# Decay attention and softplus network: the state's products in whole float32 beside the transposes

## The chip, the cores and the metric

The kernel runs on one core of a Trainium2 chip. The metric is the device time of one execution in microseconds (us). PE is the matmul engine, PEld its weight loads, ACT, DVE and POOL the scalar, vector and general engines, SP the queue that issues most transfers.

## What is computed

A causal attention with decay, by the recurrence below, feeds a two-layer network with softplus. Shapes: q, k, v are 4 x 8 heads x 768 positions x 64; the network has 3072 tokens, 512 inputs and 2048 hidden units. The weights arrive as float64, the rest as float32.

```python
for t in range(S):
    state = gamma[None, :, None, None] * state + np.einsum('bhd,bhe->bhde', k[:, :, t], v[:, :, t])
    y[:, :, t] = scale * np.einsum('bhd,bhde->bhe', q[:, :, t], state)
h = x @ w_in          # x: y with heads side by side
g = np.maximum(h, 0.0) + np.log1p(np.exp(-np.abs(h)))
out = g @ w_out
```

## The kernel before

**Units.** The recurrence is done in chunks of C = 128 positions. A unit is one chunk of one batch for half of the heads (HH = 4), so there are 4 x 6 x 2 = 48 units; `hf` is the half, `c` the chunk within a batch, NC = 6. A unit is computed as: load kn, qn, vn (128 positions on the partitions x 4 heads x 64), scale qn and vn by tables of the decay (`decay`, on POOL), transpose kn and qn on PE (`operands`, tile tp), multiply to scores sc = k q (`scores`), mask them (POOL), form y = state q + v scores (`outputs`, tile yp), and update the state: td += the sum over the chunk of k times v (`new_state`, tile pp). `stack_state` copies td into st, the form in which yp's matmuls read it. The products pp are needed for every chunk but the last of a batch: 40 of the 48 units.

**Two ways of precision.** The first WHOLE = 10 units use float32 matmuls as they are ("whole units"): pp is one matmul a head with kn as weights (64 columns) and vn as the moving operand (64 columns), L191. The other 38 ("split units", 30 of them with pp) split each operand into a high and a low float32r part and sum the products: kh is kn cast to float32r on ACT (L152), kl the rest on DVE (L153), vhl both parts of v. A head's pp is then two matmuls, kh with both parts of v (128 columns, L195) and kl with the high part (64 columns, L196). pp has a high and a low half, and td takes both on DVE, by L202 and L204.

**The network.** For each block of T = 256 tokens and each pair p of 128-wide slices of the hidden layer, `hidden` makes hp with 24 float32r matmuls (L286 to L288, xh and xl being the parts of y), ACT, DVE and POOL make the softplus parts gh and gl, and `second` adds into acc (L316 to L318). At the start each weight slice is converted from float64 words on ACT, DVE and POOL (`convert_weights`: L82, L87 and L91 on ACT, L92 on POOL).

**Order.** Units and network are interleaved by ticks: unit u has its parts at tick 4u plus an offset, by the table PARTS:

```python
PARTS = {-6: load_unit, -2: decay, 0: operands, 2: scores, 3: new_state, 5: stack_and_outputs}
```

The writing order is a hint: each engine's final order is set by a scheduler when the program is built. Each engine works through its own queue in that order and waits where an operand isn't there. tp, sc, pp and yp share three PSUM buffers of the tag "a", the network's tiles have their own.

Of the kernel before, what the change touches and what calls it, by code (L numbers as in the profile page):

```python
# [10 lines left out]
F32 = mybir.dt.float32  # L11
F32R = mybir.dt.float32r
# [3 lines left out]
ALU = mybir.AluOpType  # L16

P = 128
C = 128
# [3 lines left out]
WHOLE = 10  # L23
# [7 lines left out]
def decay_attention_then_softplus_ffn(ctx: ExitStack, tc: tile.TileContext, q, k, v, w_in, w_out, qtab, vtab, gtab, out):  # L31
    nc = tc.nc
    B, H, S, D = q.shape
    DM, DF = w_in.shape
    NC = S // C
# [3 lines left out]
    HH = H // 2  # L39
    NJ = HH // 2  # L40
# [3 lines left out]
    attn = ctx.enter_context(tc.tile_pool(name="attn", bufs=1))  # L44
# [5 lines left out]
    ps_a = ctx.enter_context(tc.tile_pool(name="ps_a", bufs=3, space=bass.MemoryType.PSUM))  # L50
# [42 lines left out]


    units = [(c // NC, c % NC, hf) for c in range(B * NC) for hf in range(2)]
    loads, live, state, xs = {}, {}, {}, {}
    lo, up = slice(0, D), slice(D, P)


# [20 lines left out]
    def operands(n):  # L120
        b, c, hf = units[n]
        kn, qn, vn = loads.pop(n)
        tp = ps_a.tile([P, 2, NJ, C], F32, name="tp", tag="a")
        for j in range(NJ):
            nc.tensor.transpose(tp[:, 0, j, :], kn[:, 2 * j:2 * j + 2, :], ident)  # L125
        for j in range(NJ):
            nc.tensor.transpose(tp[:, 1, j, :], qn[:, 2 * j:2 * j + 2, :], ident)  # L127
        if n < WHOLE:
            kw = attn.tile([P, NJ, C], F32, name="kw", tag="kh")
            qw = qws[n % 2]  # L130
            nc.scalar.copy(kw, tp[:, 0])
            nc.scalar.copy(qw[lo, 0], tp[lo, 1])
            nc.vector.tensor_copy(qw[up, 1], tp[up, 1])
            live[n] = [(kw, qw), kn, vn]
            return
        kq = kqs[n % 2]
        sides = ((0, lo, up), (1, up, lo))
        for par, own, oth in sides:
            nc.scalar.copy(kq[own, :2, par], tp[own])  # L139
            nc.scalar.copy(kq[oth, 1, par], tp[own, 1])  # L140
        for par, own, oth in sides:
            nc.vector.tensor_tensor(kq[oth, 0, par], tp[own, 0], kq[own, 0, par].bitcast(F32), op=ALU.subtract)  # L142
            nc.vector.tensor_tensor(kq[own, 2, par], tp[own, 1], kq[own, 1, par].bitcast(F32), op=ALU.subtract)

        vhl = attn.tile([P, HH, 2, D], F32R, name="vhl", tag="vhl", bufs=2)
        nc.scalar.copy(vhl[:, :, 0, :], vn)
        nc.vector.tensor_tensor(vhl[:, :, 1, :], vn, vhl[:, :, 0, :].bitcast(F32), op=ALU.subtract)
        kh = kl = None
        if c < NC - 1:
            kh = attn.tile([P, HH, D], F32R, name="kh", tag="kh")  # L150
            kl = attn.tile([P, HH, D], F32R, name="kl")
            nc.scalar.copy(kh, kn)  # L152
            nc.vector.tensor_tensor(kl, kn, kh.bitcast(F32), op=ALU.subtract)  # L153
        live[n] = [kq, vhl, kh, kl]

    def scores(n):
        kq = live[n][0]
# [23 lines left out]

    def new_state(n):
        b, c, hf = units[n]
        live[n].append(state[hf][0] if c else None)
        if c == NC - 1:
            return
        pp = ps_a.tile([D, HH, 2, D], F32, name="pp", tag="a")
        if n < WHOLE:
            kn, vn = live[n][1:3]
            for h in range(HH):  # L190
                nc.tensor.matmul(pp[:, h, 0, :], lhsT=kn[:, h, :], rhs=vn[:, h, :], start=True, stop=True)  # L191
        else:
            vhl, kh, kl = live[n][1:4]
            for h in range(HH):
                nc.tensor.matmul(pp[:, h], lhsT=kh[:, h, :], rhs=vhl[:, h], start=True, stop=False)  # L195
                nc.tensor.matmul(pp[:, h, 0, :], lhsT=kl[:, h, :], rhs=vhl[:, h, 0, :], start=False, stop=True)  # L196
        if c == 0:
            td = attn.tile([D, HH, D], F32, name=f"td{hf}")
            nc.vector.tensor_copy(td, pp[:, :, 0, :])
        else:  # L200
            td = state[hf][1]
            nc.vector.tensor_tensor(td, pp[:, :, 0, :], td, op=ALU.add)  # L202
        if n >= WHOLE:
            nc.vector.tensor_tensor(td, pp[:, :, 1, :], td, op=ALU.add)  # L204
        state[hf] = [None, td]

    def stack_state(n):
        b, c, hf = units[n]
        if c == NC - 1:
            return  # L210
        tdv = state[hf][1].rearrange("d (j p) e -> d p j e", p=2)
        if n + 2 < WHOLE:
            st = attn.tile([P, NJ, D], F32, name=f"st{hf}", bufs=2)
            nc.scalar.copy(st[lo], tdv[:, 0])
            nc.scalar.copy(st[up], tdv[:, 1])
            state[hf][0] = st
            return
        st = attn.tile([P, 2, NJ, D], F32R, name=f"st{hf}", bufs=2)
        od = attn.tile([D, NJ, D], F32R, name="od")
        nc.scalar.copy(st[lo, 0], tdv[:, 0])  # L220
        nc.scalar.copy(od, tdv[:, 1])
        nc.scalar.copy(st[up, 1], tdv[:, 1])
        nc.vector.tensor_tensor(st[up, 0], tdv[:, 0], st[lo, 0].bitcast(F32), op=ALU.subtract)
        nc.vector.tensor_tensor(st[lo, 1], tdv[:, 1], od.bitcast(F32), op=ALU.subtract)
        state[hf][0] = st

    def outputs(n):
        b, c, hf = units[n]
        kq, *rest, st = live.pop(n)
        i, off = divmod((n // 2) * C, T)  # L230
        if i not in xs:
            xs[i] = [ffn.tile([P, ND, T], F32R, name=nm) for nm in ("xh", "xl")]
        xh, xl = xs[i]
        yp = ps_a.tile([D, 2, NJ, C], F32, name="yp", tag="a")
        for j in range(NJ):
            for par in range(2):
                h = 2 * j + par
                o = yp[:, par, j, :]
                if c and n < WHOLE:
                    nc.tensor.matmul(o, lhsT=st[:, j, :], rhs=kq[1][:, par, j, :], start=True, stop=False)  # L240
                elif c:
                    nc.tensor.matmul(o, lhsT=st[:, par, j, :], rhs=kq[:, 1, par, j, :], start=True, stop=False)
                    nc.tensor.matmul(o, lhsT=st[:, par, j, :], rhs=kq[:, 2, par, j, :], start=False, stop=False)  # L243
                if n < WHOLE:
                    kn, vn, a = rest
                    nc.tensor.matmul(o, lhsT=vn[:, h, :], rhs=a[:, h, :], start=c == 0, stop=True)  # L246
                else:
                    vhl, kh, kl, ah, al = rest
                    nc.tensor.matmul(o, lhsT=vhl[:, h, 0, :], rhs=ah[:, h, :], start=c == 0, stop=False)  # L249
                    nc.tensor.matmul(o, lhsT=vhl[:, h, 0, :], rhs=al[:, h, :], start=False, stop=False)  # L250
                    nc.tensor.matmul(o, lhsT=vhl[:, h, 1, :], rhs=ah[:, h, :], start=False, stop=True)  # L251
        g = hf * NJ
        to = [(par, x[rows, g:g + NJ, off:off + C]) for x in (xh, xl) for par, rows in ((0, lo), (1, up))]
        for par, hi in to[:2]:
            nc.scalar.copy(hi, yp[:, par])  # L255
        for (par, low), (_, hi) in zip(to[2:], to[:2]):
            nc.vector.tensor_tensor(low, yp[:, par], hi.bitcast(F32), op=ALU.subtract)  # L257

    def stack_and_outputs(n):
        stack_state(n)  # L260
        outputs(n)


    PARTS = {-6: load_unit, -2: decay, 0: operands, 2: scores, 3: new_state, 5: stack_and_outputs}
    FIRST_TICK = min(PARTS)
    PERIOD = 4
    last_tick = PERIOD * (len(units) - 1) + max(PARTS)
    per_block = PERIOD * 2 * NT

    def tick(n):  # L270
        for at, part in PARTS.items():
            u, r = divmod(n - at, PERIOD)
            if r == 0 and 0 <= u < len(units):
                part(u)
# [64 lines left out]
    def ticks_for(i):  # L339

        return min(per_block * (i + 1) + max(PARTS) - PERIOD + 1 + AHEAD, last_tick + 1)

# [40 lines left out]
    for a, b in zip(starts, starts[1:]):  # L383
        i = steps[b][0]
        if i == 2:
            a = b - TURN
# [59 lines left out]
```

## Time and profile before

| | |
|---|---|
| median of 3 runs | 701.77 us (700.23 to 701.84) |
| the profiled execution | 700.03 us, span 698.2 us |
| PE busy | 684.4 us (98%) |
| DVE, ACT, POOL busy | 433.2, 372.1, 281.4 us |
| granted PE clock | full |

The span is the time from the first to the last instruction of the profiled execution. A row of the profile names the source line (L286), the engine, the operation, output tile <- input tiles, shapes and a count. In rows in order of time the first two numbers are the start and the duration in us; rows of groups end with the busy time of all and the mean duration of one in ns, then the idle time before them. A float32 matmul may show as two records. An entry like "[0.17 <-issue]" gives idle time ahead of the row and what ended it.

### The profile page before, as it was taken

What the parts mean: (1) busy time and instruction counts of PE and PEld (TensorE: products, weight loads), DVE (VectorE), ACT (ScalarE), POOL (GpSimd) and SP (SyncE); (2) the same over time, 40 slices, a digit from 0 to 9 for tenths busy, and PEclk for the clock granted to TensorE, in tenths of its full rate; (3) what the DMA queues carried; (4) which work ended last, traced back from release to release, by engine and by line L of the source; (5) the groups of instructions that cost most, each with busy time, mean ns of one, the idle gap of its engine ahead of it and who ended that gap; (6) DMA issues with size and microseconds to landing.
All of it is one profiled execution on the core that took longest, in us unless ns stands there. A gap on an engine that the chain in (4) does not pass through costs nothing.

```text
span 698.2 us, 13537 instructions
## 1 busy us (share of the span) xinstructions
PE 684.4 (98%) x5056; PEld 621.3 (89%) x5056; DVE 433.2 (62%) x893; ACT 372.1 (53%) x835; POOL 281.4 (40%) x324
## 2 busy tenths in 40 slices
PE   6899999999999999999999999999999999999997
PEld 4688889899999999999999999999999999999996
DVE  4676785557666766557667666647766676544221
ACT  6988885446556546445555555445555544543221
POOL 5676667334343342343334333433433333222221
PEclk9999999999999999999999999999999999999999
DMA  9976650122112112111111111211211110000000
GB/s 266 287 201 173 192 159 1 31 61 69 31 23 69 31 25 61 31 31 54 39 23 37 49 38 24 61 37 25 62 24 39 54 31 16 31 1 1 31 1 30
DMA packets 90752, 42.82 MB, mean 61 GB/s; under 512 B 77376, under 2 KB 85568, under 8 KB 90688
## 3 DMA queue, kind: packets, MB, share of 16 engines
q1 hardware_dynamic: 90240, 41.96, 22.2%
q8 instruction: 40, 0.66, 0.4%
q14 instruction: 24, 0.20, 0.1%
q10 hardware_dynamic: 448, 0.01, 0.0%
HBM read 35.66 MB, written 6.29 MB: 60 GB/s over the span
## 4 chain that ended last, share of the span: by engine, by line
PE 96%; ACT 1%; issue 0%; DVE 0%; ACTq 0%
PE hp L286 14%; PE hp L287 13%; PE hp L288 13%; PE acc L316 13%; PE acc L317 13%; PE acc L318 13%; PE sc L171 3%; PE tp L125 1%; PE tp L127 1%; PE pp L195 1%; PE yp L250 1%; PE yp L251 1%; PE yp L249 1%; PE yp L246 1%; PE yp L240 1%; PE yp L243 1%
## 5 line engine op out<-in xcount | busy, mean ns | idle before, releaser
L286 PE MATMUL hp<-xh,winhl 128*128 128x256 f32 x768 | 221.4, 289 | 0.4 <-ACT xh L255 0.4
L288 PE MATMUL hp<-xh,winhl 128*128 128x256 f32 x768 | 217.9, 284 | 0.0
L287 PE MATMUL hp<-xl,winhl 128*128 128x256 f32 x768 | 217.6, 283 | 0.0
L302 POOL TENSOR_TENSOR gl<-sp,gh 128x512 fp32r<-128x512 f32 x96 | 125.4, 1306 | 149.3 <-ACT gh L300 86.7
L316 PE MATMUL acc<-wouthl,gh 128*128 128x512 f32 x384 | 154.3, 402 | 0.0
L317 PE MATMUL acc<-wouthl,gh 128*128 128x512 f32 x384 | 150.4, 392 | 0.0
L318 PE MATMUL acc<-wouthl,gl 128*128 128x512 f32 x384 | 149.1, 390 | 0.0
L286 PEld LDWEIGHTS hp<-xh,winhl 128*128 128x128 f32 x768 | 146.5, 191 | 2.8 <-issue 0.5
L287 PEld LDWEIGHTS hp<-xl,winhl 128*128 128x128 f32 x768 | 147.0, 191 | 1.6 <-issue 0.5
L288 PEld LDWEIGHTS hp<-xh,winhl 128*128 128x128 f32 x768 | 146.8, 191 | 0.6 <-issue 0.3
L293 DVE TENSOR_SCALAR sp<-hp 128x512 uint32<-128x512 uint32 x96 | 66.1, 690 | 70.6 <-PE hp L288 61.0
L300 ACT CAST gh<-sp 128x512 fp32r<-128x512 f32 x96 | 59.5, 620 | 74.1 <-PE acc L317 57.4
L117 POOL TENSOR_TENSOR qn<-qn,qtabs 128x256 f32<-128x256 f32 x48 | 29.4, 613 | 151.1 <-DMA qn<-in_q_dram 125.0
L294 ACT ACTIVATE sp<-sp 128x512 f32<-128x512 f32 x96 | 60.9, 634 | 49.0 <-DVE sp L293 48.7
L318 PEld LDWEIGHTS acc<-wouthl,gl 128*128 128x128 f32 x384 | 71.9, 188 | 15.6
L316 PEld LDWEIGHTS acc<-wouthl,gh 128*128 128x128 f32 x384 | 72.4, 189 | 12.5 <-issue 0.5
L317 PEld LDWEIGHTS acc<-wouthl,gh 128*128 128x128 f32 x384 | 72.5, 189 | 11.4
L298 DVE SCALAR_TENSOR_TENSOR sp<-hp,sp 128x512 f32<-128x512 f32 x96 | 65.9, 687 | 12.8 <-ACT sp L294 11.6
L142 DVE TENSOR_TENSOR kq<-tp,kq 64x256 fp32r<-64x256 f32 x76 | 32.1, 422 | 67.0 <-ACT kq L140 65.8
L139 ACT CAST kq<-tp 64x512 fp32r<-64x512 f32 x76 | 44.1, 581 | 40.0 <-PE tp L127 38.8
L255 ACT CAST xh<-yp 64x256 fp32r<-64x256 f32 x96 | 35.1, 366 | 51.0 <-PE yp L251 44.5
L257 DVE TENSOR_TENSOR xl<-yp,xh 64x256 fp32r<-64x256 f32 x96 | 39.9, 416 | 33.7 <-ACT xh L255 32.7
(85 smaller groups left out, 1082.6 us busy)
## 6 DMA issues: line engine op xcount, KB each, us to landing
win<-in_moe_w_in_dram SPq DMA_DIRECT2D x16, 512.0 KB, 4.5
wout<-in_moe_w_out_dram SPq DMA_DIRECT2D x16, 512.0 KB, 4.4
kn<-in_k_dram SPq DMA_DIRECT2D x48, 128.0 KB, 2.3
qn<-in_q_dram SPq DMA_DIRECT2D x48, 128.0 KB, 2.8
vn<-in_v_dram SPq DMA_DIRECT2D x48, 128.0 KB, 2.2
out_dram<-o SPq DMA_DIRECT2D x24, 256.0 KB, 2.1
gtab_sb<-in_gtab_dram ACTq DMA_DIRECT2D x2, 2.0 KB, 3.8
qtabs<-in_qtab_dram ACTq DMA_DIRECT2D x1, 4.0 KB, 2.4
```

The source lines that it names most:

```text
L139: nc.scalar.copy(kq[own, :2, par], tp[own])
L286: nc.tensor.matmul(hp[:, k], lhsT=wt[:, 0, d, :], rhs=xh[:, d, :], start=d == 0, stop=False)
L287: nc.tensor.matmul(hp[:, k], lhsT=wt[:, 0, d, :], rhs=xl[:, d, :], start=False, stop=False)
L288: nc.tensor.matmul(hp[:, k], lhsT=wt[:, 1, d, :], rhs=xh[:, d, :], start=False, stop=d == ND - 1)
L293: nc.vector.tensor_scalar(sp.bitcast(U32), hps[s].bitcast(U32), 0x80000000, None, op0=ALU.bitwise_or)
L294: nc.scalar.activation(sp, sp, AF.Softplus)
L298: nc.vector.scalar_tensor_tensor(g, hps.pop(s), 0.0, g, op0=ALU.max, op1=ALU.add)
L300: nc.scalar.copy(gh, g)
L302: nc.gpsimd.tensor_tensor(gl, sps.pop(s), gh.bitcast(F32), op=ALU.subtract)
L316: nc.tensor.matmul(acc[i][t], lhsT=gh[:, k, ts], rhs=wt[:, 0], start=begins and k == 0, stop=False)
L317: nc.tensor.matmul(acc[i][t], lhsT=gh[:, k, ts], rhs=wt[:, 1], start=False, stop=False)
L318: nc.tensor.matmul(acc[i][t], lhsT=gl[:, k, ts], rhs=wt[:, 0], start=False, stop=ends and k == 1)
```

## The change

All units take the state's products from whole float32 kn and vn, one matmul a head (L132 in the new numbering). The products are written in `operands`, directly after the transposes; the td add follows in the same tick (0 in place of 3), since `new_state` is now called behind `operands`. kh, kl, the low half of pp and the second td add are gone. The state that `outputs` reads is kept in a table `prior` of its own.

```diff
+        if c < NC - 1:
+            pp[n] = ps_a.tile([D, HH, D], F32, name="pp", tag="a")
+            for h in range(HH):
+                nc.tensor.matmul(pp[n][:, h, :], lhsT=kn[:, h, :], rhs=vn[:, h, :], start=True, stop=True)
         if n < WHOLE:
-            kw = attn.tile([P, NJ, C], F32, name="kw", tag="kh")
+            kw = attn.tile([P, NJ, C], F32, name="kw")
...
-        kh = kl = None
-        if c < NC - 1:
-            kh = attn.tile([P, HH, D], F32R, name="kh", tag="kh")
-            kl = attn.tile([P, HH, D], F32R, name="kl")
-            nc.scalar.copy(kh, kn)
-            nc.vector.tensor_tensor(kl, kn, kh.bitcast(F32), op=ALU.subtract)
...
     def new_state(n):
         b, c, hf = units[n]
-        live[n].append(state[hf][0] if c else None)
+        prior[n] = state[hf][0] if c else None
         if c == NC - 1:
             return
-        pp = ps_a.tile([D, HH, 2, D], F32, name="pp", tag="a")
-        if n < WHOLE:
-            kn, vn = live[n][1:3]
-            for h in range(HH):
-                nc.tensor.matmul(pp[:, h, 0, :], lhsT=kn[:, h, :], rhs=vn[:, h, :], start=True, stop=True)
-        else:
-            vhl, kh, kl = live[n][1:4]
-            for h in range(HH):
-                nc.tensor.matmul(pp[:, h], lhsT=kh[:, h, :], rhs=vhl[:, h], start=True, stop=False)
-                nc.tensor.matmul(pp[:, h, 0, :], lhsT=kl[:, h, :], rhs=vhl[:, h, 0, :], start=False, stop=True)
...
-            nc.vector.tensor_tensor(td, pp[:, :, 0, :], td, op=ALU.add)
-        if n >= WHOLE:
-            nc.vector.tensor_tensor(td, pp[:, :, 1, :], td, op=ALU.add)
+            nc.vector.tensor_tensor(td, pp.pop(n), td, op=ALU.add)
...
+    def operands_and_state(n):
+        operands(n)
+        new_state(n)
+
-    PARTS = {-6: load_unit, -2: decay, 0: operands, 2: scores, 3: new_state, 5: stack_and_outputs}
+    PARTS = {-6: load_unit, -2: decay, 0: operands_and_state, 2: scores, 5: stack_and_outputs}
```

The change moves instructions in three places that matter here. First, PE in a split unit of the steady part. Before, the last two of the four heads' products, between other matmuls:

```order
L195 MATMUL pp<-vhl,kh 64x128
L196 MATMUL pp<-vhl,kl 64x64
L195 MATMUL pp<-vhl,kh 64x128
L196 MATMUL pp<-vhl,kl 64x64
L286 MATMUL hp<-xh,winhl 128x256
L287 MATMUL hp<-xl,winhl 128x256
```

and now:

```order
L280 MATMUL hp<-xh,winhl 128x256
L125 MATMUL tp<-ident,kn 128x128 x2
L127 MATMUL tp<-ident,qn 128x128 x2
L132 MATMUL pp<-vn,kn 64x64 x4
L308 MATMUL acc_2746<-wouthl,gh 128x512
L309 MATMUL acc_2746<-wouthl,gh 128x512
```

Eight float32r matmuls that stood by themselves have become four float32 ones between the transposes and the network's matmuls.

Second, PE among the whole units. Before, sc parts the runs of yp and pp:

```order
L318 MATMUL acc_684<-wouthl,gl 128x512
L246 MATMUL yp<-ah,vn 64x128
L163 MATMUL sc<-qw,kw 128x128 x4
L191 MATMUL pp<-vn,kn 64x64 x4
L286 MATMUL hp<-xh,winhl 128x256
```

Now pp stands directly ahead of the previous unit's yp (here its first rows), and sc by itself further on:

```order
L278 MATMUL hp<-xh,winhl 128x256
L132 MATMUL pp<-vn,kn 64x64 x4
L228 MATMUL yp<-qw,st_368 64x128
L234 MATMUL yp<-ah,vn 64x128
L228 MATMUL yp<-qw,st_368 64x128
```

pp and yp, both with 64 columns of weights, have become one run, which sc no longer parts.

Third, ACT ahead of the third pair of xh casts, which the network's first matmul needs. Before:

```order
L131 COPY kw<-tp 128x256
L132 COPY qw<-tp 64x256
L82 ACTIVATE win<-win 128x512
L91 CAST winhl<-w 128x512
L87 ACTIVATE wp<-wout 128x512
L82 ACTIVATE wout<-wout 128x512
L255 CAST xh<-yp 64x2x128 x2
```

and now:

```order
L82 ACTIVATE wout<-wout 128x512
L91 CAST wouthl<-w 128x512
L87 ACTIVATE wp<-win 128x512
L82 ACTIVATE win<-win 128x512
L201 COPY st_368<-td_183 64x128
L202 COPY st_368<-td_183 64x128
L91 CAST winhl<-w 128x512
L87 ACTIVATE wp<-wout 128x512
L82 ACTIVATE wout<-wout 128x512
L243 CAST xh<-yp 64x2x128 x2
```

More weight conversions and one more unit's st copies have moved ahead of that pair.

More of the change, by code (lines that the diff above doesn't have):

```diff
@@ L95, in decay_attention_then_softplus_ffn @@
     units = [(c // NC, c % NC, hf) for c in range(B * NC) for hf in range(2)]
-    loads, live, state, xs = {}, {}, {}, {}
+    loads, live, pp, prior, state, xs = {}, {}, {}, {}, {}, {}
     lo, up = slice(0, D), slice(D, P)
@@ L133, in operands @@
             nc.vector.tensor_copy(qw[up, 1], tp[up, 1])
-            live[n] = [(kw, qw), kn, vn]
+            live[n] = [(kw, qw), vn]
             return
@@ L147, in operands @@
         nc.vector.tensor_tensor(vhl[:, :, 1, :], vn, vhl[:, :, 0, :].bitcast(F32), op=ALU.subtract)
-        kh = kl = None
-        if c < NC - 1:
-            kh = attn.tile([P, HH, D], F32R, name="kh", tag="kh")
-            kl = attn.tile([P, HH, D], F32R, name="kl")
-            nc.scalar.copy(kh, kn)
-            nc.vector.tensor_tensor(kl, kn, kh.bitcast(F32), op=ALU.subtract)
-        live[n] = [kq, vhl, kh, kl]
+        live[n] = [kq, vhl]
     def scores(n):
@@ L183, in new_state @@
         b, c, hf = units[n]
-        live[n].append(state[hf][0] if c else None)
+        prior[n] = state[hf][0] if c else None
         if c == NC - 1:
             return
-        pp = ps_a.tile([D, HH, 2, D], F32, name="pp", tag="a")
-        if n < WHOLE:
-            kn, vn = live[n][1:3]
-            for h in range(HH):
-                nc.tensor.matmul(pp[:, h, 0, :], lhsT=kn[:, h, :], rhs=vn[:, h, :], start=True, stop=True)
-        else:
-            vhl, kh, kl = live[n][1:4]
-            for h in range(HH):
-                nc.tensor.matmul(pp[:, h], lhsT=kh[:, h, :], rhs=vhl[:, h], start=True, stop=False)
-                nc.tensor.matmul(pp[:, h, 0, :], lhsT=kl[:, h, :], rhs=vhl[:, h, 0, :], start=False, stop=True)
         if c == 0:
             td = attn.tile([D, HH, D], F32, name=f"td{hf}")
-            nc.vector.tensor_copy(td, pp[:, :, 0, :])
+            nc.vector.tensor_copy(td, pp.pop(n))
         else:
             td = state[hf][1]
-            nc.vector.tensor_tensor(td, pp[:, :, 0, :], td, op=ALU.add)
-        if n >= WHOLE:
-            nc.vector.tensor_tensor(td, pp[:, :, 1, :], td, op=ALU.add)
+            nc.vector.tensor_tensor(td, pp.pop(n), td, op=ALU.add)
         state[hf] = [None, td]
@@ L228, in outputs @@
         b, c, hf = units[n]
-        kq, *rest, st = live.pop(n)
+        kq, *rest = live.pop(n)
+        st = prior.pop(n)
         i, off = divmod((n // 2) * C, T)
@@ L244, in outputs @@
                 if n < WHOLE:
-                    kn, vn, a = rest
+                    vn, a = rest
                     nc.tensor.matmul(o, lhsT=vn[:, h, :], rhs=a[:, h, :], start=c == 0, stop=True)
                 else:
-                    vhl, kh, kl, ah, al = rest
+                    vhl, ah, al = rest
                     nc.tensor.matmul(o, lhsT=vhl[:, h, 0, :], rhs=ah[:, h, :], start=c == 0, stop=False)
```

## The prediction

> **What bounds the kernel now.** I read the page's shares first, then three stretches of the span, then the order of time on PE around the state's products.
>
> Rows of the page (busy time and share of the span of each engine; the chain that ended last, by engine):
>
> ```profile
> span 698.2 us, 13537 instructions
> PE 684.4 (98%) x5056; PEld 621.3 (89%) x5056; DVE 433.2 (62%) x893; ACT 372.1 (53%) x835; POOL 281.4 (40%) x324
> PEclk9999999999999999999999999999999999999999
> PE 96%; ACT 1%; issue 0%; DVE 0%; ACTq 0%
> ```
>
> PE's busy time in three stretches (window, its length, PE busy and its matmuls, granted clock):
>
> ```profile
> 0.00:28.00 28.00, 18.27 (x114) 1.00 1.04 282
> 28.00:690.00 662.00, 662.00 (x4927) 1.00 0.19 52
> 690.00:698.20 8.20, 4.08 (x18) 1.00 0.17 64
> ```
>
> From 28 us to 690 us PE is never idle. So the end moves by what PE's stream gains or loses there, plus any shift of the moment at which the stream becomes full; work taken from ACT and DVE (53% and 62% busy) is worth nothing by itself. A group's mean duration says little here, since matmuls overlap: a 128x256 hp lasts 0.28 us and the next starts 0.12 us later. I therefore price by starts: from the last big matmul ahead of a small group to the second big one behind it, minus the usual pace of the two (hp 0.12 us, acc 0.22 us as between its rows below).
>
> **The split units' products, before.** PE in order of time at one split unit (start, duration):
>
> ```profile
> 230.83 0.39 PE L317 MATMUL acc<-wouthl,gh 128*128 128x512 f32 x1
> 231.06 0.39 PE L318 MATMUL acc<-wouthl,gl 128*128 128x512 f32 x1
> 231.28 0.22 PE L195 MATMUL pp<-vhl,kh 128*64 128x128 f32 x1
> 231.34 0.19 PE L196 MATMUL pp<-vhl,kl 128*64 128x64 f32 x1
> 231.37 0.25 PE L195 MATMUL pp<-vhl,kh 128*64 128x128 f32 x1
> ...
> 231.69 0.19 PE L196 MATMUL pp<-vhl,kl 128*64 128x64 f32 x1
> 231.72 0.36 PE L286 MATMUL hp<-xh,winhl 128*128 128x256 f32 x1
> 231.92 0.28 PE L287 MATMUL hp<-xl,winhl 128*128 128x256 f32 x1
> ```
>
> From 231.06 to 231.92 are 0.86 us; less 0.22 and 0.12, the eight float32r matmuls of a unit cost 0.52 us. There are 30 such units:
>
> ```profile
> L195 PE MATMUL pp<-vhl,kh 128*64 128x128 f32 x120 | 17.2, 243 | 0.0
> L191 PE MATMUL pp<-vn,kn 128*64 128x64 f32 x80 | 7.4, 237 | 0.0
> ```
>
> 120 records at four a unit are 30 units; and the ten whole units' 40 float32 matmuls leave 80 records, so a whole float32 matmul runs as two passes.
>
> **The same products in whole float32.** Whole units already do what the change makes all units do. Half a unit's products (two heads, four passes) stand alone between hp matmuls, and a full unit's (eight passes) a little earlier:
>
> ```profile
> 70.56 0.28 PE L287 MATMUL hp<-xl,winhl 128*128 128x256 f32 x1
> 70.77 0.45 PE L191 MATMUL pp<-vn,kn 128*64 128x64 f32 x4
> 71.15 0.39 PE L288 MATMUL hp<-xh,winhl 128*128 128x256 f32 x1
> 71.37 0.28 PE L286 MATMUL hp<-xh,winhl 128*128 128x256 f32 x1
> ```
>
> ```profile
> 61.23 0.68 PE L191 MATMUL pp<-vn,kn 128*64 128x64 f32 x8
> ```
>
> From 70.56 to 71.37, less twice 0.12, four passes cost 0.57 us. Four more lengthen the run by 0.68 - 0.45 = 0.23 us, so a pass takes 0.058 us in the stream, and 0.57 - 0.23 = 0.34 us is a fixed toll of the run. The rows show where it falls: pp starts 0.21 us after hp instead of 0.12, the first hp behind it comes late, and the second follows after 0.22 instead of 0.12. A unit's eight passes then cost 0.57 + 0.23 = 0.80 us where the float32r group costs 0.52.
>
> The change puts them behind the transposes, which are float32 too. Does that spare the toll? The nearest rows have transposes followed at once by one float32 matmul of 64 columns of weights (yp), two passes:
>
> ```profile
> 27.70 0.51 PE L286 MATMUL hp<-xh,winhl 128*128 128x256 f32 x2 [0.37 <-ACT xh L255]
> 28.04 0.39 PE L125 MATMUL tp<-ident,kn 128*128 128x128 f32 x2
> 28.26 0.38 PE L127 MATMUL tp<-ident,qn 128*128 128x128 f32 x2
> 28.57 0.43 PE L240 MATMUL yp<-qw,st 128*64 128x128 f32 x2
> 28.93 0.38 PE L287 MATMUL hp<-xl,winhl 128*128 128x256 f32 x1
> 29.16 0.28 PE L288 MATMUL hp<-xh,winhl 128*128 128x256 f32 x1
> ```
>
> A pair of transposes takes 0.22 us (28.04 to 28.26), so yp would start at 28.48 and starts at 28.57; its pair takes 0.43 where a transposes' pair takes 0.38, 0.05 more; hp behind it is 0.09 late (0.36 between the two starts, 0.22 for two passes and the 0.05), and the next comes 0.23 later instead of 0.12. Together 0.34 us: the full toll. It goes with 64-column float32 weights, not with float32 as such; a float32 score matmul with 128 columns pays none (40.10 to 40.44 is two passes of 0.11 and one hp of 0.12):
>
> ```profile
> 40.10 0.38 PE L163 MATMUL sc<-qw,kw 128*128 128x128 f32 x2
> 40.24 0.36 PE L288 MATMUL hp<-xh,winhl 128*128 128x256 f32 x1
> 40.44 0.28 PE L286 MATMUL hp<-xh,winhl 128*128 128x256 f32 x1
> ```
>
> So a split unit's group goes from 0.52 to 0.80 us: 30 x 0.28 = **+8.4 us**, all in the stretch where PE is full. Ends: 30 x (0.46 - 0.52) = -1.8 if behind the transposes only the eight passes of 0.058 counted, and +8.4 with the full toll. I take +8.4, since the yp rows show the very transition.
>
> Weight loads show the toll's place: float32r weights load one matmul early, the float32 ones of yp only with their own matmul.
>
> ```profile
> 231.06 0.13 PEld L195 LDWEIGHTS pp<-vhl,kh 128*64 128x64 f32 x1
> 28.57 0.19 PEld L240 LDWEIGHTS yp<-qw,st 128*64 128x64 f32 x2 [0.17 <-issue]
> ```
>
> The Trainium skill ("TensorE: Matmul & The Clock Gate", the step on LDWEIGHTS) says that the queue pulls weight loads ahead, so that the next tile's weights load while this tile's matmul runs. By that rule the product's first load would hide behind the transposes and the split units would gain a little (the rival "no toll"). The float32r row agrees with it, the yp row does not.
>
> **Whole units.** Their matmuls are the same, but their runs join: before, pp mostly stood behind sc, which ends one 64-column run and begins another; now it stands next to yp, and the two are one run. The order lists 23 runs of 64-column float32 matmuls after the first hp and up to the last whole unit's yp before, and 12 now. 11 x 0.34 = **-3.7 us**. Ends: 0, if PE's gaps there are set by waits, and -3.7; PE is full there, so I take the whole.
>
> **The start.** The first hp (27.70 above) needs the third pair of xh casts, and ACT reaches it late: in the new order 48 ACT instructions stand from the first kw copy up to that pair, before 40 (six more weight conversions, two more st copies). ACT's stretch before, its first row and its end, with two conversions in a row:
>
> ```profile
> 5.91:26.90 20.99, 17.76 (x40) 1.00 1.15 314
> ```
>
> ```profile
> 5.91 0.37 ACT L131 COPY kw<-tp 128x256 f32<-128x256 f32 x1 [3.81 <-PE tp L127]
> ...
> 24.73 0.63 ACT L87 ACTIVATE wp<-wout 128x512 uint32<-128x512 uint32 x1
> 25.30 0.67 ACT L82 ACTIVATE wout<-wout 128x512 f32<-128x512 f32 x1
> 26.90 0.74 ACT L255 CAST xh<-yp 64x256 fp32r<-64x256 f32 x2 [0.93 <-PE yp L246]
> ```
>
> Conversions follow each other at 0.57 us (24.73 to 25.30); with 0.3 for an st copy, an estimate, eight more are 6 x 0.57 + 2 x 0.3 = 4.0 us. ACT is idle for 20.99 - 17.76 = 3.2 us there, which could absorb as much: +0.8 to +4.0. One more unit's transposes (2 x 0.22) are by then behind PE, so +0.4 to +3.6. On PE each pp now stands ahead of the previous unit's yp and of its own sc, and waits for its vn; on POOL the second unit's vn now stands behind a weight subtraction:
>
> ```profile
> 11.88 1.28 POOL L92 TENSOR_TENSOR winhl<-w,winhl 128x512 fp32r<-128x512 f32 x1
> ```
>
> That may add 1.3, so the end is +4.9; I take **+2.5**, near the middle, as such a wait keeps part of ACT's idle time alive. PE cannot give this back later, being full.
>
> **At nothing.** Gone are, per split unit, kh (ACT), kl and one of the two td adds (DVE); PE's full stretch covers them, and if it didn't, ACT and DVE would be faster, not slower. The td add comes three ticks earlier and needs the st copies of two units ago, which were issued three ticks earlier still. kn and vn are kept no longer than the end of pp or yp, so the loads on SP's queue keep their distance; tp, pp, yp and two sc share three PSUM buffers as before, five allocations a unit, which in the steady part stand 96 rows of PE's order apart from the next unit's. The last two units have no product, and the tail after 690 us stays.
>
> **Sum.** 8.4 - 3.7 + 2.5 = +7.2 us on the profiled execution's 700.03 us: 707.2. That execution is 1.7 below the median of the runs (701.77) and beside the fastest (700.23); for a median I add half of it, **708.1 us**.
>
> **Rivals.**
> - *No toll behind transposes.* The place is the first pass of pp behind tp, the price 30 x 0.34; it decides if PE runs tp and pp as one float32 stretch. Sum -1.8 - 3.7 + 2.5 = -3.0: 697.0 and, as a median, 697.9, faster. For it: transposes and products are both float32 from the same kn. Against it: the 28.57 row. With half the toll, 30 x 0.17 = 5.1 come back, and the kernel is within 0.3% of before.
> - *No gain in the whole units, and a start that waits fully.* The scheduler's order has one whole unit's last head parked far behind its first three, and pp now waits in PE's queue. +8.4 + 4.9 - 0 = +13.3: about 714. For it: ACT is 85% busy ahead of the first hp; against it: PE is full from 28 us on, so the tolls there are not waits.
> - *A start that loses nothing.* ACT's idle 3.2 us takes up the conversions: 8.4 - 3.7 + 0.4 = +5.1: 706 as a median.
>
> **Chances.** Forecast (+5.5 to +10) 0.62; the start without loss 0.18; whole units without gain 0.10; no toll 0.06 and half the toll 0.04. About 0.3% (2.1 us) is what a measurement of this kernel tells from no change. So slower 0.90, same 0.04, faster 0.06. The range takes the forecast, both starts and most of the whole-unit rival: 703.5 to 713.
>
> **What would show it.** In the new profile: pp as 320 records of 64 columns; behind each second transposes' pair a gap of 0.09 us, eight passes in 0.46 us, and acc twice 0.1 late, 0.80 us in all. If acc follows after the usual pace the toll step is wrong. The first hp comes near 30.6 us instead of 27.70 (the start), with PE full from then on, and 12 tolls instead of 23 up to the last whole unit's yp. The prediction fails if the toll is shared with the transposes, or if a wait appears on PE inside the full stretch.

## The result and the profile after

The changed kernel takes 708.76 us (median of 4 runs, 708.19 to 709.15); the kernel before took 701.67 us beside it. The ratio is 1.0105 with a 95% interval of [1.0088, 1.0123]: slower by 1%, and 0.7 us above the forecast of 708.1. The profiled execution took 708.19 us, 8.16 more than that of before. Beside this run and the experiments the kernel before took 699.9 to 700.4 us in some executions and 701.2 to 702.5 us in the others; its profiled execution (700.03) is of the first kind, so a difference from it comes out larger than one between medians.

The page of the changed kernel, the same rows as of before:

```profile
span 706.5 us, 13405 instructions
PE 689.5 (98%) x5056; PEld 625.2 (88%) x5056; DVE 394.8 (56%) x833; ACT 358.0 (51%) x805; POOL 279.9 (40%) x324
PE 94%; ACT 1%; DVE 0%; issue 0%; ACTq 0%
```

DVE has 38 us less to do and ACT 14, and the span is 8.3 us longer: on engines with a third or half of their time free the saving bought nothing. PE busy rose by 5.1 us; the other 3.2 us are idle time, which the stretches place (window, length, PE busy, DVE, ACT and POOL after PEld, granted clock):

```profile
0.00:28.00 28.00, 15.44 (x96) 12.71 (x97) 14.09 (x35) 20.78 (x44) 17.62 (x32) 0.91 1.04 281
28.00:690.00 662.00, 661.47 (x4896) 601.92 (x4895) 377.93 (x795) 334.49 (x757) 259.68 (x291) 1.00 0.19 52
```

From 28 us on PE is as good as full: 0.53 us of its 662 are idle, where before none were. Ahead of that it does 15.44 us of work instead of 18.27, at a granted clock of 0.91 instead of 1.00, so some 2.8 us of the added idle time lie there.

One split unit of the changed kernel, PE in order of time (start, duration):

```profile
236.63 0.28 PE L280 MATMUL hp<-xh,winhl 128*128 128x256 f32 x1
236.75 0.38 PE L125 MATMUL tp<-ident,kn 128*128 128x128 f32 x2
236.97 0.38 PE L127 MATMUL tp<-ident,qn 128*128 128x128 f32 x2
237.28 0.68 PE L132 MATMUL pp<-vn,kn 128*64 128x64 f32 x8
237.89 0.50 PE L308 MATMUL acc<-wouthl,gh 128*128 128x512 f32 x1
238.22 0.39 PE L309 MATMUL acc<-wouthl,gh 128*128 128x512 f32 x1
238.45 0.39 PE L310 MATMUL acc<-wouthl,gl 128*128 128x512 f32 x1
```

After the second pair of transposes pp would start at 237.19 and starts at 237.28: 0.09 us. From pp to acc are 0.61 us where eight passes of 0.058 are 0.46, so 0.15 more, and from the first acc to the second 0.33 instead of 0.23. Together the 0.34 of the toll. From 236.63 to 238.22, less one hp (0.12) and one acc (0.23), tp and pp cost 1.24 us; tp alone costs 0.44, so pp costs 0.80. All 160 matmuls show as two records each, and the first weight load of a unit's pp (PEld) starts only with its matmul:

```profile
L132 PE MATMUL pp<-vn,kn 128*64 128x64 f32 x320 | 28.3, 233 | 5.4 <-POOL vn L118 4.5 <-DVE xl L245 0.5 <-POOL qn L117 0.2
237.28 0.54 PEld L132 LDWEIGHTS pp<-vn,kn 128*64 128x64 f32 x8 [0.17 <-issue]
```

### The profile page after: what moved, and what is told of

Its sections match the earlier page's. It is cut to its first block, busy times and chain, and to the rows that moved or that the text cites. A ratio compares the mean times of both kernels' runs of the same rounds, so it can differ in the third digit from the quotient of the medians.

```text
span 706.5 us, 13405 instructions
## 1 busy us (share of the span) xinstructions
PE 689.5 (98%) x5056; PEld 625.2 (88%) x5056; DVE 394.8 (56%) x833; ACT 358.0 (51%) x805; POOL 279.9 (40%) x324
## 4 chain that ended last, share of the span: by engine, by line
PE 94%; ACT 1%; DVE 0%; issue 0%; ACTq 0%
PE acc L308 13%; PE hp L278 13%; PE hp L279 13%; PE hp L280 13%; PE acc L309 12%; PE acc L310 12%; PE pp L132 3%; PE sc L170 3%; PE yp L237 1%; PE tp L125 1%; PE tp L127 1%; PE yp L238 1%; PE yp L239 1%; PE yp L230 1%; PE yp L231 1%; PE yp L228 1%
## 5 line engine op out<-in xcount | busy, mean ns | idle before, releaser
L176 POOL TENSOR_SCALAR_AFFINE_SELECT ah<-ah 128x512 fp32r<-128x512 f32 (+1 forms) x48 | 30.5, 635 | 85.5 <-DVE al L173 76.6
```

## The experiments

Each was compared with the kernel before on the same chip; for e1 to e4 that was at 701.45 us, for e5 to e7, on another chip, at 701.27. In the diffs, "..." and comments stand for code left out.

### e1: the precision alone

```diff
-    PARTS = {..., 0: operands_and_state, 2: scores, 5: ...}
+    PARTS = {..., 0: operands, 2: scores, 3: products_and_state, 5: ...}
     # products: the four float32 matmuls of a unit, moved out of operands
```

> Precision alone: the products of all units are whole float32, but stay at tick 3 as in the kernel before, away from the transposes. PE's order up to the tenth unit is that of before. Theory (a toll of 0.34 us of every run of 64-column float32 matmuls, whatever stands beside it): the 30 split units cost 0.80 instead of 0.52 us each, the start and the whole units are as before: 8.4 us over the kernel before, about 710.1, the first hp near 27.7 us. Rival (what the changed kernel lost comes from the place next to the transposes: the wait for vn in PE's queue and the order there): within 2 us of the kernel before.

Measured: 709.1 us, ratio 1.0109 [1.0091, 1.0127], 7.6 us over the kernel before. The products stand by themselves between other matmuls, and a unit's group reads:

```profile
234.05 0.39 PE L314 MATMUL acc<-wouthl,gh 128*128 128x512 f32 x1
234.28 0.39 PE L315 MATMUL acc<-wouthl,gl 128*128 128x512 f32 x1
234.60 0.68 PE L184 MATMUL pp<-vn,kn 128*64 128x64 f32 x8
235.21 0.39 PE L283 MATMUL hp<-xh,winhl 128*128 128x256 f32 x1
235.43 0.28 PE L284 MATMUL hp<-xl,winhl 128*128 128x256 f32 x1
```

From 234.28 to 235.43 are 1.15 us, less 0.23 and 0.12: 0.80, the same as behind the transposes. So the split units lose through the format, wherever they stand. The rival, that the place does it, is out. The total fell 1.0 us short of the theory's 710.1, and the first hp came at 29.35 us where 27.7 was expected (the last section shows why). From the first hp to the end of the span, which leaves the start out, the profiled execution of e1 takes 679.45 us and that of the kernel before 670.50: 8.95 more, with 8.4 expected.

### e2: the place alone

```diff
+        if n < WHOLE and c < NC - 1:      # in operands, behind the transposes
+            pp = pps[n] = ps_a.tile([D, HH, 2, D], F32, name="pp", tag="a")
+            for h in range(HH):
+                nc.tensor.matmul(pp[:, h, 0, :], lhsT=kn[:, h, :], rhs=vn[:, h, :], start=True, stop=True)
     # split units as before: kh, kl and vhl at tick 3
```

> Place alone: the ten whole units' products stand next to the transposes as in the changed kernel, the split units keep their float32r products with kh and kl at tick 3. Theory: the start loses 3.4 us as in the changed kernel (first hp near 31.5 us), 12 runs of 64-column float32 matmuls stand where 23 stood, 11 x 0.34 = -3.7; together about -0.3: 701.4, no change. Rival (the joined runs save nothing, as the gaps were waits): +3.4, 705.1. Rival (the start's loss belongs to the split units' change): -3.7, 698.

Measured: 701.09 us, ratio 0.9997 [0.9987, 1.0006]: no change. The start is lost as in the changed kernel (the first hp is at 32.31 us, where 31.5 was expected), although the split units are as before, so the rival that the split units' change delays it is out. Something of about the same size must have come back in the whole units. Eleven tolls less, 3.7 us, are of that size; had the joined runs saved nothing, 705.1 was to be expected. The trace shows it directly. Counted from the first hp to the last whole unit's yp, the kernel before has 23 runs of 64-column float32 matmuls, e2 and the changed kernel have 12 each. One joined run of e2:

```profile
49.32 0.68 PE L132 MATMUL pp<-vn,kn 128*64 128x64 f32 x8
49.84 0.38 PE L244 MATMUL yp<-qw,st 128*64 128x128 f32 x2
...
51.37 0.38 PE L250 MATMUL yp<-ah,vn 128*64 128x128 f32 x2
51.68 0.39 PE L300 MATMUL hp<-xl,winhl 128*128 128x256 f32 x1
51.90 0.28 PE L301 MATMUL hp<-xh,winhl 128*128 128x256 f32 x1
```

Between pp and yp nothing is lost: 0.52 us for eight passes and the first pass's 0.05. From the first hp to the end of the span are 667.09 us against 670.50 before. Of the 3.41 us gained 0.44 are transposes that now stand ahead of the first hp; the other 3.0 are what the whole units save, less 0.4 us of waits that PE did not have there before.

### e3: the first four units back at tick 3

```diff
+LATE = 4
+        if n >= LATE:        # in operands, behind the transposes
+            products(n)
+    # units below LATE: products(n) and new_state(n) at tick 3
```

> The changed kernel with the products of the first four units back at tick 3, all else as changed; the order up to the first hp is that of before. Theory: the first hp comes at 27.7 us again and the start's 3.4 us are gone; 11 runs of 64-column float32 matmuls where 23 stood, -4.1; split units +8.4: +4.3 over the kernel before, 706.0. Rival (the late first hp was a delay that other work used up, so nothing comes back): as the changed kernel, 708.8.

Measured: 705.85 us, ratio 1.0063 [1.0047, 1.008]: 4.4 us over the kernel before, where 4.3 was expected, and 2.9 less than the changed kernel's 708.76 (which ran on another occasion; by the two ratios it is also 2.9). Of the 2.9, 0.34 is one toll fewer (11 against 12), so some 2.6 us are the start. The first hp is at 28.91 us where 27.7 was expected; in this profiled execution the granted clock was 0.53 from 24 to 26 us, as in the one of e1 that the last section shows.

### e4: who sets the first hp?

```diff
-        nc.gpsimd.tensor_tensor(vn, vn, vtabs[...], op=ALU.mult)
+        if n != 3:
+            nc.gpsimd.tensor_tensor(vn, vn, vtabs[...], op=ALU.mult)
```

In the changed kernel PE stands still for 3.15 us ahead of the fourth unit's pp, for vn on POOL (start, duration, idle time before and what ended it):

```profile
22.17 0.44 PE L127 MATMUL tp<-ident,qn 128*128 128x128 f32 x2 [0.43 <-POOL qn L117]
25.77 0.78 PE L132 MATMUL pp<-vn,kn 128*64 128x64 f32 x8 [3.15 <-POOL vn L118]
...
31.52 0.50 PE L278 MATMUL hp<-xh,winhl 128*128 128x256 f32 x2
```

That looks like the cause of the late first hp. This kernel takes the wait away.

> The changed kernel, but the fourth unit's v is not scaled by the decay table (this part of the computation is left out), so that its product waits for the load alone and not for POOL. PE's order up to the first hp is unchanged, on ACT one instruction less stands ahead of the third pair of xh casts. Theory A (the start's loss is PE's wait for vn on POOL and the half clock that follows it): pp of that unit starts near 22.7 us instead of 25.8, at full clock, first hp near 28 us, 705.5 in all. Theory B (the loss is ACT's longer queue ahead of the xh casts, as predicted; PE would wait there anyway): first hp at 30 to 31 us, 707.5 to 708.8.

Measured: 710.23 us, ratio 1.0125 [1.0107, 1.0143], slower still than the changed kernel. In its PE rows 0.71 us are left of the wait, and another stands ahead of the first hp:

```profile
23.65 0.65 PE L133 MATMUL pp<-vn,kn 128*64 128x64 f32 x8 [0.71 <-ACT win L82]
...
27.19 0.38 PE L128 MATMUL tp<-ident,qn 128*128 128x128 f32 x2
31.20 0.50 PE L279 MATMUL hp<-xh,winhl 128*128 128x256 f32 x2 [3.62 <-ACT xh L244]
```

pp starts 2.1 us earlier, and the first hp only 0.3, since it waits 3.62 us for xh on ACT. Theory B holds for the first hp: ACT's queue sets it. The third pair of xh casts, in the changed kernel and then in e4, shows the same:

```profile
30.75 0.72 ACT L243 CAST xh<-yp 64x256 fp32r<-64x256 f32 x2
30.41 0.74 ACT L244 CAST xh<-yp 64x256 fp32r<-64x256 f32 x2
```

They end at 31.47 and 31.15 us, and the first hp starts 0.05 us later each time. In the changed kernel PE's own transposes end their 0.22 us at 31.22, so its queue is only 0.3 us behind ACT's. The time of 710.23 us lies above the ranges of both theories. PE's stretches there (window, length, busy, clock) show a reason:

```profile
27.00:31.00 4.00, 0.57 (x6) 1.00 1.00 297
31.00:35.00 4.00, 3.04 (x17) 0.68 0.86 219
35.00:39.00 4.00, 4.00 (x31) 0.89 0.53 153
```

PE is now idle just ahead of the hp stream, and the clock falls at the stream's beginning, where time lost is not won back. In the changed kernel the half clock fell on work ahead of the first hp, in time that PE would have waited for ACT anyway. The same two matmul groups behind the first hp, in the changed kernel and then in e4, place the 1.5 us:

```profile
32.23 0.65 PE L132 MATMUL pp<-vn,kn 128*64 128x64 f32 x8 [0.20 <-POOL qn L117]
34.41 0.43 PE L234 MATMUL yp<-ah,vn 128*64 128x128 f32 x2
32.46 1.08 PE L133 MATMUL pp<-vn,kn 128*64 128x64 f32 x8 [0.76 <-ACT ah L164]
36.15 0.43 PE L235 MATMUL yp<-ah,vn 128*64 128x128 f32 x2
```

From pp to yp are 2.18 us in the one and 3.69 in the other, 1.5 more, where the clock is low. A wait of 0.76 us instead of 0.20 ahead of pp adds 0.6, the earlier first hp takes off 0.3, and some 0.2 come back behind. The next unit's pp is at 41.29 and 42.79 us, 1.50 apart, as far as the spans are (706.5 and 708.0).

### e5, e6, e7: the toll without the 64 columns

```diff
-            pp[n] = ps_a.tile([D, HH, D], F32, name="pp", tag="a")
-            for h in range(HH):
-                nc.tensor.matmul(pp[n][:, h, :], lhsT=kn[:, h, :], rhs=vn[:, h, :], start=True, stop=True)
+            pp[n] = ps_a.tile([P, NJ, P], F32, name="pp", tag="a")
+            for j in range(NJ):
+                nc.tensor.matmul(pp[n][:, j, :], lhsT=kn[:, 2 * j:2 * j + 2, :], rhs=vn[:, 2 * j:2 * j + 2, :], start=True, stop=True)
...
+        for rows in (lo, up):      # td is now [P, NJ, D]: even heads below, odd heads above
+            own = new[rows, :, rows]
...
+                nc.vector.tensor_tensor(td[rows], own, td[rows], op=ALU.add)
```

The st copies follow the new layout of td: whole units need one on ACT instead of two, split units one less. e5 has this at the changed kernel's place, e6 at tick 3, e7 at tick 3 for the first four units and behind the transposes for the rest.

> The changed kernel with two float32 matmuls of head pairs per unit instead of four of single heads: weights of 128 columns (k of two heads) and 128 moving columns (v of the same two), of which the two diagonal blocks are used; td keeps even heads in the lower and odd heads in the upper partitions. Theory (the toll belongs to 64-column float32 weights): 4 passes of 0.109 and no toll, 0.44 us a unit instead of 0.80; 30 split units 2.4 us below the kernel before; 11 runs of 64-column float32 matmuls after the first hp where 23 stood, -4.1; the start +3.4 as in the changed kernel: 698.4 in all. Rival (the toll belongs to real float32 matmuls of any width behind transposes): 0.78 a unit, 708.3.

> The same pairs at tick 3, as in the kernel before. Theory: split units -2.4, 14 runs after the first hp where 23 stood, -3.1, the start as before: 5.5 below the kernel before, 696.0. Rival (toll for any real float32 matmul): 30 x 0.26 - 0 = +7.8, 709.3.

> Pairs, the first four units at tick 3 and the others next to the transposes. Theory: -2.4 for the split units, 11 runs after the first hp where 23 stood, -4.1, the start as before: 6.5 below the kernel before, 695.0. Rival (the start's loss follows the pairs too, since ACT's queue ahead of the xh casts is set anew): 695 plus up to 3.4, 698.4.

Measured: e5 698.51 us, 0.9965 [0.9953, 0.9977]; e6 696.15 us, 0.993 [0.9916, 0.9944]; e7 696.03 us, 0.9931 [0.9918, 0.9944]. All three are faster than the kernel before. A unit of e5:

```profile
235.53 0.38 PE L125 MATMUL tp<-ident,kn 128*128 128x128 f32 x2
235.75 0.38 PE L127 MATMUL tp<-ident,qn 128*128 128x128 f32 x2
235.96 0.61 PE L132 MATMUL pp<-vn,kn 128*128 128x128 f32 x4
236.33 0.48 PE L307 MATMUL acc<-wouthl,gh 128*128 128x512 f32 x1
236.65 0.39 PE L308 MATMUL acc<-wouthl,gh 128*128 128x512 f32 x1
```

pp follows tp at once (235.75 plus 0.22), and acc follows pp as it follows the transposes in a unit without products. The float32 matmul is as real as before and half of what it computes is thrown away, yet the unit's products take 0.45 instead of 0.80 us on PE. From 235.75 to 236.65 are 0.90: 0.22 of transposes, 0.23 of acc, 0.45 of pp. The pairs are also half as many matmuls with twice the moving columns, but neither explains it: the yp row of the prediction, one matmul of two passes with 128 moving columns on 64 columns of weights, pays the full 0.34. So the toll belongs to float32 weights of 64 columns, and the rival for any float32 matmul is out. e5 keeps the start's loss (its first hp is at 33.24 us) and e6 loses it (28.01 us). e7 gains nothing over e6, where 1.0 was expected, and the intervals overlap. Neither the start nor the count of runs fell short: the first hp of e7 is at 26.71 us, 1.0 earlier than before, and from there to the last whole unit's yp the traces have 11 runs in e7 and 14 in e6, as expected. But PE waits behind the first hp, 2.3 us in e7 (1.27 of them at one unit's pp, for vn on POOL) and 1.6 in e6, where e5 waits 0.15 and the kernel before nothing. The theory left these waits out, and they are of the size of what is missing: the profiled execution of e7 is 4.8 us below that of before, with 6.5 expected.

## Why the prediction was right, point by point

- *Split units, +8.4.* 0.80 us a unit as priced from the yp rows, 30 x 0.28. e1 confirms it by itself and without the place, at 7.6 between medians and 8.95 from the first hp to the end.
- *The toll is not shared with the transposes.* Right: 0.09, 0.15 and 0.10 in the rows. In the new profile the first weight load of pp is not hidden: it starts with its matmul at 237.28 us. The LDWEIGHTS rule of the Trainium skill ("TensorE: Matmul & The Clock Gate", the step on LDWEIGHTS) would have hidden it behind the transposes; for these weights the measurement decides against that. The Trainium skill ties the pulling ahead, in the same step, to row groups that do not conflict or to the background weight buffer; no run here shows whether these conditions hold.
- *Whole units, -3.7.* The count of 23 and 12 runs stands in the traces. e2 comes out even with a start lost, and 3.0 us shorter behind the first hp; e3 is at +4.4 against 8.4 - 4.1 = 4.3. PE does wait for 0.4 us behind the first hp of the changed kernel (0.20 for qn on POOL, 0.18 for xl on DVE), a sign that the prediction named for its failing, but too small to matter.
- *The start, +2.5.* The mechanism was right. By medians e3 gives 2.6; that 2.5 comes so near is in part luck, as it was taken from the middle of 0.4 to 4.9. Between the two profiled executions the size is larger. ACT from its first kw copy to the third xh pair, of the changed kernel and then of the kernel before (window, length, ACT busy):

```profile
5.70:30.75 25.05, 21.74 (x49) 0.86 1.13 317
```

```profile
5.70:26.90 21.20, 17.77 (x40) 1.00 1.15 314
```

ACT is idle for 3.31 us in the one and 3.43 in the other. The prediction let that idle time absorb part of the eight added instructions (0.8 to 4.0); on balance it absorbed nothing, and they cost their full 3.97 us of busy time. The wait of 0.93 us for PE's yp just ahead of the pair is gone, but waits of 0.89 and 0.48 us for DVE have come in further up. The first hp moved by 3.82 us, less 0.44 for the transposes done early: +3.4, or 0.9 more than the term. Part of this goes back to the kernel before's profiled execution, which ran at full clock there: with the same order up to the first hp, e1 and e3 had it at 29.35 and 28.91 us. The added wait for vn, priced at up to 1.3, was there on PE (4.5 us in all) and cost 0.3 us of the first hp by itself (e4).
- *Sum.* With 3.4 in the place of 2.5 the sum is 8.1 against 8.16 measured between the profiled executions. From the first hp to the end are 674.98 us against 670.50; with the 0.44 of transposes that is 4.9 more, where 8.4 - 3.7 = 4.7 was forecast. For medians the forecast added 0.85 us; the changed kernel's median lies 0.57 above its profiled execution. The start, 0.9 short, and this addition, 0.3 too large, leave the forecast 0.7 below the median.
- *Work taken from ACT and DVE, nothing.* Right: 52 us less, and no trace of it in the time.

## What to carry to other kernels

On a kernel whose PE is full, price a change in matmuls by start-to-start times around a small group, with its neighbours, and not by mean durations: the cost here was in the entry to and the exit from a format and a width of weights. Look for the same transition elsewhere in the trace before believing that neighbours share it; and if half-width float32 weights pay such a toll, filling them with a second head and discarding the cross terms can be the cheapest way (696 us here). At a kernel's start, count the instructions ahead of the one that gates the stream on the engine that issues it; a wait seen on another engine may be cover for that queue.

## What the runs showed of the hardware that was not expected

Two things. First, float32 weights of 128 columns, transposes, scores and pairs alike, enter and leave the stream of float32r matmuls with next to no cost (e5's pairs take 0.45 us, and four passes of 0.109 are 0.44), while 64 columns cost 0.34 us a run. Why they do, no run shows. Second, the granted clock at the start differs between executions of the same order. The kernel before, and then e1, whose PE order up to there is the same (window, length, PE busy, clock):

```profile
22.00:24.00 2.00, 0.73 (x5) 1.00 1.16 295
24.00:26.00 2.00, 2.00 (x16) 1.00 1.21 299
```

```profile
22.00:24.00 2.00, 0.81 (x5) 1.00 1.15 294
24.00:26.00 2.00, 1.94 (x8) 0.53 1.21 293
```

After the same sparse stretch one execution goes on at full clock and the other at about half, with 8 matmul records where the first has 16. The first hp is at 29.35 us in e1 against 27.70 in the kernel before. A change of under 2 us in this kernel can thus not be read from one pair of profiles, the 0.9 us of the start above included.
